# Moving the scores of one tile between the sums of the last image pair, transposing half of two lines unadded, and loading the last line as 120 and 8 partitions

## The chip, the cores and the metric

The kernel runs on one core of one Trainium2 chip. The metric is the device time of one execution in microseconds (us).

## The reference, cut to what matters

```python
# attention: q is 4 x 12288 x 128, kv is an image 4 x 384 x 32 x 128, r = 4
kv_pool = kv.reshape(B, H // r, r, W // r, r, C).mean(axis=(2, 4))   # 768 keys per batch
k = v = kv_pool.reshape(B, -1, C) @ w_sr
s = (q @ k.transpose(0, 2, 1)) / sqrt(C)
a = softmax(s)
x = a @ v
# feed-forward: d_ff = 1536
out = (maximum(x @ w_gate, 0) * (x @ w_val)) @ w_out
```

The pooling takes 4 x 4 pixels into one key. Each batch has 768 keys, which the kernel handles as three pairs of 128. A pair is loaded as four "lines" (the four pixel rows of the pooling window), each a copy of 128 partitions by 4096 bytes. Queries come in tiles of 512.

## The kernel before

TensorE pools and transposes at once: it transposes the pixels in float32 and accumulates the transposes in PSUM. VectorE halves the number of transposes by adding two lines first.

```python
def kv_load(b, pair):
    parts = work.tile([128, r, 2, r, C], FP32, tag="kv_in", bufs=3)
    rows = kv[b, pair * 2 * HC : (pair + 1) * 2 * HC].rearrange(
        "(hp dh) (wp h dw) c -> dh hp wp (h dw c)", dh=r, h=2, dw=r)
    for dh in range(r):                                   # four lines, 512 KiB each
        nc.sync.dma_start(parts[:, dh].rearrange("p h dw c -> p (h dw c)"), rows[dh])
    kv_in[b, pair] = parts

def turn_add(b, pair, lines, first=False, final=False, chunks=(0, 1)):
    n = lines.shape[2]
    for h in chunks:                                      # h: the two halves (128 keys each)
        for i in range(n):                                # four float32 transposes, accumulated
            nc.tensor.matmul(kv_Ts[b, pair][:, h], lines[:, h, i], ident, is_transpose=True, ...)
    if final and h == 1:                                  # copy from PSUM for the projection
        nc.vector.tensor_copy(kvT, kv_Ts[b, pair])
# ... cut ...
idle = bank([128, 128])                                   # warm-up of TensorE
for _ in range(34):
    nc.tensor.matmul(idle, ident16, ident16, start=True, stop=True)
# ... cut: tile 0, first pair of keys, start of the second pair ...
for k in range(GRP):                                      # four tiles of queries
    for jc in range(2, 4):
        scores(k, jc)                                     # second pair of keys
    if k == 0:
        turn_values(0, 1)
    if k == 1:
        turn_open(0, 2)                                   # third, last pair
        turn_add(0, 2, s2, first=True)                    # its lines 0 and 1, added before
        for h in range(2):                                # its lines 2 and 3, half by half
            s2 = add_lines(2, 2, nc.vector, slice(h, h + 1))
            turn_add(0, 2, s2, final=True, chunks=[h])
    if k == 2:
        project(0, 2)
attend(0, 1)
attend(1, 1)
for jc in range(4, NJC):
    scores(0, jc)                                         # third pair of keys
turn_values(0, 2)
for jc in range(4, NJC):
    scores(1, jc)
# ... cut: values of tile 0, its normalization, scores of tiles 2 and 3, x_turn_pe(0) ...
# ... then the steady loop: value, gate and output projections of one tile
#     beside the attention of a later one, to the end ...
```

The softmax here doesn't subtract the row's maximum and nothing guards it: scores larger than these inputs give would overflow.

## Time and profile before

| | before |
|---|---|
| device time, median of 6 runs | 1048.48 us (1047.68 to 1049.20) |
| the profiled execution | 1048.43 us, span 1046.4 us |
| TensorE busy | 1036.4 us, 99% of the span |
| from the first value projection (32.82 us) to the end | 1013.6 us |

The table says where a change can act: from 32.82 us on, TensorE is the bound (busy for 1009.47 of 1013.61 us), and the opening before it is 3% of the time. The prediction below shows the lines of the opening.

To compare openings between executions I use three marks from each trace. **A** is the start of the eight float32 transposes of the last pair's first two lines (22.62 in the prediction's timeline); up to there all kernels of this study do the same, apart from the warm-up where that is said. **B** is the last semaphore update of that pair's second line. **L** is the last update of its last line. (In these traces a 128-partition line has sixteen updates by DMA, for the second line of the profiled execution of before from 19.25 to 19.89 us. I call what one update reports a share, and read it as the part of one of the core's sixteen DMA engines: while only late shares were missing, from 22 to 23 us there, the DMA share is 0.06, about one of sixteen. "Fetch" is the transfer of the 16384-byte instruction block that the prediction shows.) The start of the first value projection, counted from A, is the length of the opening that the change can alter.

### The profile page before, as it was taken

The page shows a single profiled execution, that of the slowest core. Times are in us where ns is not written, and L with a number is a line of the kernel's source. Part 1 is how long each engine was busy: PE and PEld are TensorE (multiplying, and loading weights), DVE is VectorE, ACT ScalarE, POOL GpSimd, SP SyncE. Part 2 cuts the span into 40 slices and gives each one's busy share as a digit, 9 for nine tenths or more (in the row PEclk, how much of TensorE's full clock was granted, in tenths as well). Part 3 has the DMA queues.
Part 4 walks back from the last instruction along what each step waited for, and adds up shares of the span by engine and source line. Part 5 has one row for each costly group of instructions (what it writes and reads, how often), then busy time and mean ns, then how long its engine had stood idle before and what let it go on. Part 6 is the DMA issues. An engine that isn't in the chain of part 4 may idle for free.

```text
span 1046.4 us, 25971 instructions
## 1 busy us (share of the span) xinstructions
PE 1036.4 (99%) x9980; PEld 691.1 (66%) x9980; DVE 913.8 (87%) x1680; ACT 908.5 (87%) x1741; POOL 107.6 (10%) x127
## 2 busy tenths in 40 slices
PE   7999999999999999999999999999999999999998
PEld 6566666666666666666666666666666666666665
DVE  3788889898888888898888888889988888888898
ACT  2988888888888888888888888888888888888887
POOL 2000045200000015500000003430000000000000
PEclk9999999999999999999999999999999999999999
DMA  8833256231322335523224134551331322212111
GB/s 302 119 81 69 70 191 162 57 87 32 84 54 62 76 122 140 154 62 72 54 64 87 31 87 132 147 152 40 78 65 53 72 63 55 67 32 67 32 47 47
DMA packets 125853, 90.75 MB, mean 87 GB/s; under 512 B 103328, under 2 KB 104224, under 8 KB 125728
## 3 DMA queue, kind: packets, MB, share of 16 engines
q1 hardware_dynamic: 120288, 75.85, 26.8%
q0 software_dynamic: 5440, 13.24, 7.7%
q8 instruction: 78, 1.28, 0.5%
q14 instruction: 47, 0.39, 0.1%
HBM read 52.76 MB, written 25.17 MB: 74 GB/s over the span
## 4 chain that ended last, share of the span: by engine, by line
PE 97%; DMA 2%; SPq 0%; DVE 0%; ACT 0%; issue 0%; DVEq 0%; ACTq 0%
PE bank_ps L255 25%; PE bank_ps L234 24%; PE bank_ps L245 24%; PE bank_ps L196 12%; PE bank_ps L185 12%; DMA parts<-in_kv_dram 1%; DMA q<-in_q_dram 1%; PE bank_ps L166 0%; PE bank_ps L154 0%; SPq L128 0%; ACT val L238 0%; PE bank_ps L174 0%; PE bank_ps L227 0%; DVE kv_s L343 0%; DVE rinv L204 0%
## 5 line engine op out<-in xcount | busy, mean ns | idle before, releaser
L248 DVE SCALAR_TENSOR_TENSOR hT<-bank_ps,val 128x512 f16<-128x512 f32 x1152 | 759.6, 686 | 100.9 <-ACT val L238 74.5
L238 ACT CAST val<-bank_ps 128x512 f16<-128x512 f32 x1152 | 677.8, 591 | 112.1 <-PE bank_ps L234 107.5
L255 PEld LDWEIGHTS <-hT 128*128 128x128 f16 x4608 | 351.4, 98 | 199.9 <-issue 0.4
L255 PE MATMUL bank_ps<-wo,hT 128*128 128x128 f16 x4608 | 443.2, 219 | 0.0
L234 PE MATMUL bank_ps<-xT,wv 128*128 128x512 f16 x1152 | 436.6, 379 | 0.1
L245 PE MATMUL bank_ps<-xT,wg 128*128 128x512 f16 x1152 | 435.7, 378 | 0.1
L186 ACT ACTIVATE aT<-bank_ps 128x512 f16<-128x512 f32 x576 | 346.3, 605 | 18.4 <-PE bank_ps L185 18.4
L196 PE MATMUL bank_ps<-kv,aT 128*128 128x129 f16 x2304 | 223.3, 219 | 0.0
L196 PEld LDWEIGHTS <-aT 128*128 128x128 f16 x2304 | 177.3, 98 | 68.4 <-issue 0.4
L185 PE MATMUL bank_ps<-qT,kv 128*128 128x512 f16 x576 | 216.4, 379 | 1.5 <-DVE kv L167 0.8
L245 PEld LDWEIGHTS <-wg 128*128 128x128 f16 x1152 | 111.5, 97 | 66.1 <-issue 1.0
L234 PEld LDWEIGHTS <-wv 128*128 128x128 f16 x1152 | 112.7, 98 | 0.4 <-issue 0.4
L212 DVE TENSOR_TENSOR x<-bank_ps,rinv 128x256 f16<-128x256 f32 x188 | 79.7, 424 | 6.7 <-DVE rinv L204 0.2
L78 POOL DMA_DIRECT2D q<-in_q_dram x23 | 12.5, 543 | 571.8 <-DMA qT<-q 571.5
L273 DVE TENSOR_SCALAR o_sb<-bank_ps 128x512 f32<-128x512 f32 (+1 forms) x95 | 64.0, 673 | 1.3 <-PE bank_ps L255 1.3
L137 POOL TENSOR_TENSOR s<-parts 128x512 f32<-128x512 f32 x36 | 45.3, 1270 | 162.7 <-DMA parts<-in_kv_dram 122.3
L185 PEld LDWEIGHTS <-kv 128*128 128x128 f16 x576 | 55.9, 98 | 2.4 <-DVE kv L167 1.4
L204 DVE RECIPROCAL rinv<-bank_ps 128x2 f32<-128x2 f32 x192 | 30.5, 159 | 1.2 <-PE bank_ps L196 1.2
L139 POOL TENSOR_TENSOR s<-s 128x512 f32<-128x512 f32 x18 | 22.8, 1268 | 1.4
L141 POOL TENSOR_TENSOR c<-s 128x256 f32<-128x256 f32 x18 | 13.0, 725 | 1.4
L161 DVE COPY kvT<-bank_ps 128x256 f32<-128x256 f32 x12 | 5.0, 415 | 7.2 <-PE bank_ps L154 7.2
L154 PE MATMUL bank_ps<-ident,kv_s 128*128 128x128 f32 x50 | 7.8, 275 | 1.6 <-DVE kv_s L343 1.6
(37 smaller groups left out, 83.3 us busy)
## 6 DMA issues: line engine op xcount, KB each, us to landing
parts<-in_kv_dram SPq DMA_DIRECT2D x48, 512.0 KB, 6.1
out_dram<-o_sb SPq DMA_DIRECT2D x95, 256.0 KB, 2.1
q<-in_q_dram POOLq DMA_DIRECT2D x23, 512.0 KB, 5.2
xT<-x SPq DMA_TRANSPOSE x94, 2.5
q<-in_q_dram SPq DMA_DIRECT2D x1, 768.0 KB, 7.9
wv<-in_moe_w_val_dram POOLq DMA_DIRECT2D x2, 192.0 KB, 4.6
wg<-in_moe_w_gate_dram POOLq DMA_DIRECT2D x2, 192.0 KB, 5.1
wo<-in_moe_w_out_dram POOLq DMA_DIRECT2D x1, 384.0 KB, 9.9
```

Source lines behind the costliest of these rows:

```text
L137: eng.tensor_tensor(s2[:, i], parts[:, 2 * i, h], parts[:, 2 * i + 1, h], op=ALU.add)
L185: nc.tensor.matmul(s_ps, kv16[:, k // NST, jc, 0:C], qT_of(k), start=True, stop=True)
L186: nc.scalar.activation(aTs[k][:, jc, :], s_ps, AF.Exp, scale=qk_scale)
L196: nc.tensor.matmul(x_ps[:, i, :], aTs[k][:, jc, s * 128 : (s + 1) * 128], kv16[:, k // NST, jc, C : 2 * C + 1], start=(jc == 0 and i == 0) ...
L204: nc.vector.reciprocal(rinvs[k, half], x_banks[k, half][:, :, C : C + 1])
L212: nc.vector.tensor_tensor(x16s[k][:, 2 * half : 2 * half + 2, :], x_ps[:, :, 0:C], rinv.to_broadcast([128, 2, C]), op=ALU.mult,)
L234: nc.tensor.matmul(va_ps, wv16[:, fb * 128 : (fb + 1) * 128], xTs[k], start=True, stop=True)
L238: nc.scalar.copy(val, va_ps)
L245: nc.tensor.matmul(g_ps, wg16[:, fb * 128 : (fb + 1) * 128], xTs[k], start=True, stop=True)
L248: nc.vector.scalar_tensor_tensor(hTs[k][:, fb, :], g_ps, 0.0, vals.pop((k, fb)), op0=ALU.max, op1=ALU.mult)
L255: nc.tensor.matmul(o_ps, hTs[k][:, fb, s * 128 : (s + 1) * 128], wo16[:, fb, :], start=first, stop=(fb == NFB - 1), skip_group_check=True,)
L273: nc.vector.tensor_scalar(o_sb, o_ps, 1.0 / X_SCALE**2, None, op0=ALU.mult)
```

## The change: intent and diff

TensorE stood idle for 1.10 us while it waited for the last line, although scores of tiles 2 and 3 were ready to run. The new order puts the scores of tile 2 ahead of those sums and the scores of tile 3 after them. It also transposes one half of the last two lines raw, so that this half needs no VectorE addition first, and puts the values of tile 1 behind its scores. The split of the last line is meant to take work from one DMA engine: 120 partitions, then 8.

```diff
         for dh in range(r):
-            nc.sync.dma_start(parts[:, dh].rearrange("p h dw c -> p (h dw c)"), rows[dh])
+            whole = parts[:, dh].rearrange("p h dw c -> p (h dw c)")
+            if (b, pair, dh) == (0, NJC // 2 - 1, r - 1):
+                cut = 2 * HC // r - 2
+                nc.sync.dma_start(whole[: 4 * cut], rows[dh][:cut])
+                nc.sync.dma_start(whole[4 * cut :], rows[dh][cut:])
+            else:
+                nc.sync.dma_start(whole, rows[dh])
# ... cut: the loop over k shown above goes; scores_of(k, pair) is scores of both its blocks ...
+    scores_of(0, 1)
+    turn_values(0, 1)
+    scores_of(1, 1)
+    turn_open(0, 2)
+    turn_add(0, 2, s2, first=True)
+    scores_of(2, 1)
+    turn_add(0, 2, line(2, 2), chunks=[0])
+    turn_add(0, 2, line(2, 3), chunks=[0], final=True)
+    turn_add(0, 2, add_lines(2, 2, nc.vector, slice(1, 2)), chunks=[1], final=True)
+    scores_of(3, 1)
+    project(0, 2)
     attend(0, 1)
-    attend(1, 1)
-    for jc in range(4, NJC):
-        scores(0, jc)
+    scores_of(0, 2)
     turn_values(0, 2)
-    for jc in range(4, NJC):
-        scores(1, jc)
+    scores_of(1, 2)
+    attend(1, 1)
     attend(0, 2)
```

More of the change, by code (lines that the diff above doesn't have):

```diff
@@ L384, with scores_of @@
     project(0, 1)
-    for k in range(GRP):
-        for jc in range(2, 4):
+    def scores_of(k, pair):
+        for jc in (2 * pair, 2 * pair + 1):
             scores(k, jc)
-        if k == 0:
-            turn_values(0, 1)
-        if k == 1:
-            turn_open(0, 2)
-            turn_add(0, 2, s2, first=True)
-            for h in range(2):
-                s2 = add_lines(2, 2, nc.vector, slice(h, h + 1))
-                turn_add(0, 2, s2, final=True, chunks=[h])
-        if k == 2:
-            project(0, 2)
+    scores_of(0, 1)
[9 more added lines that the diff above has]
+    project(0, 2)
     attend(0, 1)
+    scores_of(0, 2)
+    turn_values(0, 2)
+    scores_of(1, 2)
     attend(1, 1)
-    for jc in range(4, NJC):
-        scores(0, jc)
-    turn_values(0, 2)
-    for jc in range(4, NJC):
-        scores(1, jc)
     attend(0, 2)
@@ L409 @@
         keep_values(0, half)
-    for jc in range(4, NJC):
-        scores(2, jc)
+    scores_of(2, 2)
     x_turn_pe(0)
-    for jc in range(4, NJC):
-        scores(3, jc)
+    scores_of(3, 2)
     attend(1, 2)
```

## The prediction

> **What bounds the kernel now.** First I read the busy shares and the chain that ended last on the profile page.
>
> ```profile
> PE 1036.4 (99%) x9980; PEld 691.1 (66%) x9980; DVE 913.8 (87%) x1680; ACT 908.5 (87%) x1741; POOL 107.6 (10%) x127
> PE 97%; DMA 2%; SPq 0%; DVE 0%; ACT 0%; issue 0%; DVEq 0%; ACTq 0%
> ```
>
> TensorE has work for 1036.4 of 1046.4 us and is 97% of the chain. Windows over 50 to 1000 us show it busy without a gap. So the time is TensorE's list of work plus the holes in it, about 10 us, and nearly all of these lie in the first 44 us. A change of the opening can win only holes. Next I read the chain of waits from 20 to 33.3 us, the part that the change touches.
>
> ```profile
> 12.22 11.65 DMA parts<-in_kv_dram
> ...
> 24.00 0.70 DVE kv_s L343
> 24.70 0.04 issue
> 24.75 1.27 PE bank_ps L154 x8
> ...
> 26.04 0.44 DVE kvT L161
> ...
> 26.61 0.67 PE bank_ps L166 x2
> 27.28 0.43 PE bank_ps L185 x2
> 27.71 0.91 PE bank_ps L196 x16
> 28.62 0.23 PE bank_ps L185
> ```
>
> Here the chain leaves TensorE: the last image line lands at 23.88, VectorE adds its first half (0.70), TensorE sums it (eight float32 transposes in two halves), VectorE copies, TensorE projects at 26.61. The timeline of TensorE shows the hole in front of those sums, in brackets:
>
> ```profile
> 22.62 1.03 PE L154 MATMUL bank_ps<-ident,kv_s 128*128 128x128 f32 x8
> 24.75 1.26 PE L154 MATMUL bank_ps<-ident,kv_s 128*128 128x128 f32 x8 [1.10 <-DVE kv_s L343]
> 25.84 0.59 PE L185 MATMUL bank_ps<-qT,kv 128*128 128x512 f16 x2
> 26.61 0.67 PE L166 MATMUL bank_ps<-kvT,w_sr_f 128*128 128x256 f32 x2 [0.18 <-DVE kvT L161]
> ```
>
> 1.10 us idle (it counts a drain; by starts TensorE is free at 23.49, so 1.26 us), while the scores of tiles 2 and 3, whose inputs were ready at 22, stand behind the sums in program order. Last, why does the line land so late? Windows of half a microsecond:
>
> ```profile
> 21.00:21.50 0.50, 0.17 (x1) 0.11 (x2) 0.27 (x1) 0.00 (x0) 0.50 (x1) 1.00 0.89 360
> 21.50:22.00 0.50, 0.50 (x5) 0.31 (x4) 0.00 (x0) 0.25 (x1) 0.50 (x2) 1.00 0.23 74
> 22.00:22.50 0.50, 0.36 (x3) 0.01 (x1) 0.29 (x1) 0.50 (x2) 0.50 (x2) 1.00 0.07 16
> 22.50:23.00 0.50, 0.50 (x5) 0.50 (x5) 0.00 (x0) 0.50 (x2) 0.50 (x2) 1.00 0.06 25
> ```
>
> The last two columns are the DMA share and GB/s. From 22 to 23 us the share is 0.06, one engine of sixteen: one straggler. The DMA view of 20.5 to 22 us has the reason, a packet of another queue:
>
> ```profile
> q8 instruction: 1, 0.02, 4.5%
> ```
>
> That packet (16384 bytes) starts at 20.63 and takes 1.08 us, where the 4096-byte rows take 0.16. By the semaphore updates, fifteen shares of the third line are there by 21.17 and the sixteenth at 22.80; of the last line fifteen by 22.41 and the sixteenth at 23.88.
>
> [...] The trace of before only has 128-partition copies, with 16 updates each[...]. [...] the trace shows one slow engine but not its number. [...] 78 packets of 16384 bytes on that queue, and by about 20 us TensorE has run some 256 instructions; so the straggler should come back at the same place. [...] Here the split is meant to drop one engine[...].
>
> **The change, part by part.** Everything up to TensorE's 23.49 us keeps its order (the build's lists confirm it). GpSimd and ScalarE keep their lists; SyncE gets one more load, VectorE one add of 0.69 less, TensorE four float32 transposes more (eight of raw lines replace four of sums for one half). Steps taken from starts in the trace: a pair of scores 0.43, four transposes 0.44 (0.109 each), eight value matmuls 0.45, the projection 0.51 to the next start.
>
> Split. Without it the last line stays at 23.88. With it the 120 rows are there by about 22.41, and two engines carry 4 more rows at 0.16 each: about 23.0 (estimate). The third line's straggler (22.80) stays. The extra issue waits for a load that landed at 13.49, long before.
>
> New order from 23.49: scores of tile 2 to 23.92; four transposes of the third line (landed 22.80) to 24.36; four of the last line to 24.80, which need it by 24.36; meanwhile VectorE adds the second half, 24.00 to 24.70 even with the line at 23.88; four transposes of that sum to 25.24. So TensorE should not wait for the image at all, and **the split is worth about nothing once the order is changed**: a line at 23.88 is still 0.4 us early for the direct transposes, and the add is just in time (24.75 against 24.80). It only buys a margin.
>
> Then: scores of tile 3 to 25.70, the copy from PSUM 25.46 to 25.90 (last transpose start plus 0.31 as before), projection at 26.04 against 26.61: 0.57 won. That is 1.26 of hole plus 0.17 of the small wait between the halves, less 0.44 for the added transposes and less 0.43, because only one pair of scores is now left after the sums to cover the copy, as before; the two scores of tile 2 had to be done anyway.
>
> After the projection, before had scores (0.43) and two value groups (0.91) and reached the scores of the last pair at 28.46. Now only one value group (0.45) is left there: free at 27.00, but the new keys are scaled at 27.17 (projection plus 1.13, from the rows of before), so a wait of 0.23 and a start at 27.23. The bank wait behind the first exponential (0.5 us in before) stays, so the block to the end of tile 1's scores is as long as before, 28.51; then the moved value group of tile 1, 0.45, and tile 0's group starts at 28.96 against 29.74, about 0.8 won. From there both orders are alike: sums, turn of tile 0, scores of tile 3, and the first value projection at about 32.0 against 32.82. ScalarE has twelve exponentials in this stretch at about 0.49; it now starts at 23.90 rather than 26.25, so it is no new bound. Weights land by 29.78, the next tile's transposed queries at 39.28, needed past 41.5: early enough.
>
> From 33 us on the list is the same and bound by TensorE, so the 0.8 us should reach the end: 1048.71 - 0.8 = 1047.9.
>
> **Rivals.** (a) *The straggler decides.* [...] it gets four rows more: line at about 24.5, add done 25.2, sums end 0.5 later, and 0.3 is won: 1048.4. [...] (b) *The holes move.* The waits for the copy, the projection and the banks come back elsewhere (before 33 us TensorE's holes after 23.49 sum to only about 2.4, and 0.44 of work is added); scores in flight hold banks that the next ones want. Against: the build's waits there are for exponentials done by 24.5. Value: 1048.5 to 1048.7. (c) *Earlier start, later stall.* From 42 to 50 us ScalarE is 100% busy and sets the pace. If it were tied to absolute time, the gain would be given back there; but its exponentials come forward by the same 0.8, so I expect it to shift. Value if wrong: 1048.7. (d) *The split is worth its full 1 us besides*, if unprofiled runs straggle worse than the profiled one: 1047.0.
>
> **Range and chances.** The whole hole is below 0.3% of the time; 2% would need 21 us, which no part of this stage holds. The three runs of before spread by 0.95 us, as much as the effect, and another chip or moment can shift by as much. Hence 1047.9, 1046.8 to 1048.9, with 99% within 2%.
>
> **What would show it.** Right: the hole of 1.10 before the float32 transposes is gone and no wait of TensorE for image lines over 0.1 us remains; TensorE's projection starts near 26.0; the scores of the last pair near 27.2; first value projection near 32.0; a span near 1045.6. Right on the split: fewer than 0.1 us change if it is undone. Wrong: a new wait of over 0.4 us on the exponentials' banks, or the first value projection unchanged, or moved but with the span unchanged (rival c), or the last line landing after 24.4 (rival a).

## The result, and the profile after

The change ran at a median of 1048.36 us (1047.77 to 1049.01, six runs) against 1048.48 us (1047.68 to 1049.20, six runs) for the kernel before. The ratio is 1.0000, with a 95% interval of 0.9987 to 1.0013: the same. Ratios here and below are the mean time of one kernel's fast runs over the mean of the other's of the same rounds, so not quite the ratio of the medians.

This first line of the profile page of the changed kernel answers to the one of before; each engine has its busy us, share of the span and instructions:

```profile
PE 1036.4 (99%) x9984; PEld 690.5 (66%) x9984; DVE 913.9 (87%) x1679; ACT 908.9 (87%) x1741; POOL 107.6 (10%) x127
```

TensorE has its four transposes more, VectorE one addition less, and the busy times are the same within 0.6 us. The span of this execution is 1047.1 us. Next is the chain of waits of the changed kernel in the opening (start, duration, what):

```profile
13.12 12.24 DMA parts<-in_kv_dram
25.55 0.70 DVE kv_s L349
26.30 0.67 PE bank_ps L160 x4
27.00 0.44 DVE kvT L167
27.57 0.68 PE bank_ps L172 x2
```

The chain still runs through the last image line, as before: the line, VectorE's addition, the sums, the copy, the projection. In the timeline of TensorE of the changed kernel (start, duration, group, and in brackets the idle time before it):

```profile
23.42 1.04 PE L160 MATMUL bank_ps<-ident,kv_s 128*128 128x128 f32 x8
24.29 0.59 PE L191 MATMUL bank_ps<-qT,kv 128*128 128x512 f16 x2
24.72 1.34 PE L160 MATMUL bank_ps<-ident,parts 128*128 128x128 f32 x8
26.30 0.66 PE L160 MATMUL bank_ps<-ident,kv_s 128*128 128x128 f32 x4 [0.24 <-DVE kv_s L349]
...
27.57 0.67 PE L172 MATMUL bank_ps<-kvT,w_sr_f 128*128 128x256 f32 x2 [0.18 <-DVE kvT L167]
...
33.52 0.38 PE L240 MATMUL bank_ps<-xT,wv 128*128 128x512 f16 x1
```

The hole of 1.10 us is gone, and a small one of 0.24 us is left; the eight raw transposes take 1.34 us where eight others take 1.04, which is another 0.3 us of waiting. A is at 23.42, 0.80 us later than in the profiled execution of before, and the projection and the first value projection are later too. From A to the first value projection it is 10.10 us, against 10.20 before. The rest, from there to the end, is 1013.57 against 1013.62 us.

So in this pair of traces the gain of 0.8 us did not arise at all. The line came late again. The last update of the second line, B, is at 20.80; of the last line the 120-partition copy has fourteen shares at 22.65 to 24.30 and its fifteenth at 25.36, and the 8-row piece is there, in two shares, at 24.91. Fifteen and two are the numbers that the split was built on. L is thus 4.56 us behind B, longer than the 3.99 us of before. These windows of the changed kernel (the last two columns are the DMA share and GB/s) show it:

```profile
21.00:22.00 1.00, 0.61 (x2) 0.20 (x2) 0.94 (x2) 0.00 (x0) 1.00 (x1) 1.00 0.94 213
22.00:23.00 1.00, 0.87 (x5) 0.42 (x6) 0.19 (x2) 0.45 (x1) 1.00 (x2) 1.00 0.67 193
23.00:24.00 1.00, 0.86 (x8) 0.71 (x7) 0.17 (x1) 1.00 (x3) 1.00 (x3) 1.00 0.20 66
```

From 21 to 22 us the DMA engines are 94% busy and move only 213 GB/s; in the window before it was 356. In the packets of the trace a 4096-byte row of this copy takes 0.2 to 0.3 us and up to 0.49, where it takes 0.16 in the 128-partition lines. Then one engine is left over again: it fetched an instruction block of 16384 bytes at 22.07 (1195 ns) and had seven rows of the last line still to do after it.

### The profile page after: what moved, and what is told of

It is laid out like the page before. It is cut to its first block, busy times and chain, and to the rows that moved or that the text cites. A ratio compares the mean times of both kernels' runs of the same rounds, so it can differ in the third digit from the quotient of the medians.

```text
span 1047.1 us, 25980 instructions
## 1 busy us (share of the span) xinstructions
PE 1036.4 (99%) x9984; PEld 690.5 (66%) x9984; DVE 913.9 (87%) x1679; ACT 908.9 (87%) x1741; POOL 107.6 (10%) x127
## 4 chain that ended last, share of the span: by engine, by line
PE 97%; DMA 2%; SPq 0%; DVE 0%; ACT 0%; issue 0%; DVEq 0%; ACTq 0%
PE bank_ps L261 25%; PE bank_ps L240 24%; PE bank_ps L251 24%; PE bank_ps L202 12%; PE bank_ps L191 12%; DMA parts<-in_kv_dram 1%; DMA q<-in_q_dram 1%; PE bank_ps L172 0%; PE bank_ps L160 0%; SPq L134 0%; ACT val L244 0%; PE bank_ps L180 0%; PE bank_ps L233 0%; DVE kv_s L349 0%; DVE rinv L210 0%
## 5 line engine op out<-in xcount | busy, mean ns | idle before, releaser
L150 POOL TENSOR_TENSOR kv_s<-c 128x128 f32<-128x128 f32 x18 | 8.2, 454 | 1.4
```

## The experiments

All kernels gave the right result.

**The parts alone, and an attempt to move the fetch.** My theory after the result was that the new order works, that the split is harmful, and that an instruction fetch of TensorE delays one DMA engine. The rival was that the order itself gains nothing. Four kernels were timed on one chip, with nine runs of before at a median of 1048.20 us.

The order alone, from the changed kernel:

```diff
-            (the split of the last line)
+            nc.sync.dma_start(parts[:, dh].rearrange("p h dw c -> p (h dw c)"), rows[dh])
```

> The new order with the last line loaded as 128 partitions. Two marks make runs comparable whose image stream starts earlier or later: A, the start of the eight float32 sums of the third pair's first two lines (22.62 us before, 23.42 after the change), and B, the last update of that pair's second line (19.89 before, 20.80 after). Theory 1 (the order is worth its 0.8 us, and the split took it back by landing the line late): the last line ends about 4.0 us behind B as before (4.56 with the change), no hole of TensorE over 0.25 us before the last sums, the first value projection starts about 9.4 us behind A (10.2 before, about 10.2 after the change), the time 0.8 us below before. Theory 2 (the holes only move, the split is neutral): the first value projection stays 10.2 us behind A and the time as before.

Measured: 1047.95 us (1047.65 to 1048.15), ratio 0.9994 (0.9981 to 1.0008). The timeline of TensorE with the order alone:

```profile
24.24 1.04 PE L154 MATMUL bank_ps<-ident,parts 128*128 128x128 f32 x8
25.23 0.66 PE L154 MATMUL bank_ps<-ident,kv_s 128*128 128x128 f32 x4
...
32.45 0.38 PE L234 MATMUL bank_ps<-xT,wv 128*128 128x512 f16 x1
```

A is at 22.94 and L at 24.36, 4.05 us behind B, as late as in the profiled execution of before. TensorE nevertheless waits for no line: no bracket stands before the sums. The first value projection is 9.51 us behind A. By starts, the last four transposes come 0.99 us behind the eight raw ones, where the second and third trace of the change have 0.87, so some 0.12 us of waiting is left. This is the case that the prediction worked out, and in the opening the order does what was expected. The 0.8 us expected in the total is not shown: the median is 0.25 us lower and the interval holds 1.

The split alone, in the kernel before:

```diff
-            nc.sync.dma_start(parts[:, dh].rearrange("p h dw c -> p (h dw c)"), rows[dh])
+            (the split of the last line)
```

> The old order with the last line as 120 and 8 partitions. Theory 1 (the split lands the line later): fifteen shares of the 120 rows spread over more than 1.2 us and their packets take 0.2 to 0.3 us rather than 0.16; last update about 4.5 us behind B; first value projection about 10.7 us behind A; time about 0.5 us above before. The change's own intent (the split avoids the delayed engine): last update about 3.1 us behind B, first value projection about 9.3 behind A, time about 0.9 us below before.

Measured: 1049.23 us (1048.48 to 1049.70), ratio 1.0006 (0.9994 to 1.0019). The interval holds 1, so a loss in the total is not shown. The timeline of TensorE with the split alone:

```profile
25.20 1.26 PE L160 MATMUL bank_ps<-ident,kv_s 128*128 128x128 f32 x8 [1.07 <-DVE kv_s L349]
...
33.28 0.38 PE L240 MATMUL bank_ps<-xT,wv 128*128 128x512 f16 x1
```

The hole that the split could have removed is 1.07 us, against 1.10 before. L is 3.79 us behind B, and the first value projection 10.18 us behind A (23.10). The split gains nothing in this trace. Neither expectation is met: L lies between the 3.1 and the 4.5 us expected.

A warm-up with fewer instructions, in the kernel before. In the prediction's trace the fetch comes after some 256 instructions of TensorE, so I expected that 25 fewer warm-up matmuls, each wider, would move it behind the lines. (Each matmul counts twice, as a weight load and a matmul, of which the page of before lists 9980 each, so this is 50 instructions.)

```diff
-    idle = bank([128, 128])
-    for _ in range(34):
-        nc.tensor.matmul(idle, ident16, ident16, start=True, stop=True)
+    fill = const.tile([128, T], FP16)
+    nc.vector.memset(fill, 1.0)
+    idle = bank([128, T])
+    for _ in range(9):
+        nc.tensor.matmul(idle, ident16, fill, start=True, stop=True)
```

> The kernel before, with the 34 warm-up matmuls of 128 columns replaced by 9 of 512 columns: 50 TensorE instructions fewer ahead of the image lines, about the same time of warm-up. If the late share of the last two lines comes from TensorE's own instruction block of 16384 bytes, which is fetched at about its 261st recorded instruction in both traces, the fetch comes behind the image stream (near 26 us), all shares of the last line land within 0.7 us, about 2.5 us behind B, and the first value projection comes about 8.7 us behind A; time 1.4 us below before. If one engine is slow by itself, the last line stays about 4.0 us behind B and the time as before.

Measured: 1047.76 us (1047.54 to 1049.28), ratio 0.9996 (0.9984 to 1.0009). The fetch did not go to 26 us as expected: it is at 21.32, when TensorE had started 206 recorded instructions, against 256 in the first trace of before. So the first block does not wait for the 256th. That the blocks are TensorE's fits their number (78 for 19960 recorded instructions of TensorE in before, 256 to each), and the third to fifth start at nearly the same instructions in both kernels (685, 941, 1197 in before, 695, 943, 1207 here). But the fetch came behind that engine's image rows, and no share of the line was late: L is 2.51 us behind B. The 1.4 us expected in the total is not shown. The timeline of TensorE with the old order and the wide warm-up:

```profile
23.07 2.00 PE L154 MATMUL bank_ps<-ident,kv_s 128*128 128x128 f32 x16
...
25.68 0.67 PE L166 MATMUL bank_ps<-kvT,w_sr_f 128*128 128x256 f32 x2 [0.18 <-DVE kvT L161]
...
31.89 0.38 PE L234 MATMUL bank_ps<-xT,wv 128*128 128x512 f16 x1
```

All sixteen transposes run in one piece, and the first value projection is 8.82 us behind A. With an early line the old order is shorter than the new order's 9.3 to 9.5.

The new order with the wide warm-up, without the split (the two edits above together):

> The new order, one load of 128 partitions, and the 9 wide warm-up matmuls. If TensorE no longer waits for the line in the new order, an earlier line brings it nothing: first value projection about 9.4 us behind A as in the run with the order alone, so 0.7 us later than with the old order and wide warm-up, because the four added float32 transposes and the moved value group stand in it for nothing. If the new order still waits for the line, it gains with the earlier line and comes under 9.0.

Measured: 1048.07 us (1047.96 to 1048.67), ratio 0.9998 (0.9985 to 1.0010). L is 2.49 us behind B, 1.56 us earlier than with the order alone, and the first value projection is 9.34 us behind A. An earlier line brings the new order little (9.51 to 9.34): it hardly waits for it any more.

**What the split does to the copy, and on which engine the fetch runs.** These were one look each, beside a run of before at 1047.89 us; they were run for their traces.

The whole change with the wide warm-up:

> The whole change plus the 9 wide warm-up matmuls, so that the fetch of the instruction block no longer stands in the image stream. If the 120 rows are slow by themselves, their packets take 0.2 to 0.3 us and the last line ends 3.6 to 3.9 us behind B, where the same order with one 128-partition load and wide warm-up had 2.5; the first value projection comes about 9.4 us behind A all the same, since the new order waits for nothing before 1.4 us behind A. If the fetch had made the line late in the changed kernel, it now ends about 2.6 us behind B.

Measured: 1048.27 us, 9.33 us from A to the first value projection. The fetch came after the rows of its engine. Yet L, with the 8-row piece, is 3.73 us behind B, where the unsplit line with the same order and warm-up had 2.49. So in this pair of traces the split copy lands over a microsecond later by itself, without a fetch among its rows. The new order hides that here.

The change once more, with no edit:

> The changed kernel itself once more, for a second trace. If the late line of the first trace is typical, the last line ends 3.8 to 4.6 us behind B, the fifteen shares of the 120 rows spread over more than 1.2 us, and the first value projection comes 9.6 to 10.1 us behind A. If it was one bad execution: about 3.1 behind B and 9.4 behind A.

Measured: 1047.85 us. The timeline of TensorE of this second trace of the change:

```profile
23.06 1.03 PE L160 MATMUL bank_ps<-ident,kv_s 128*128 128x128 f32 x8
23.93 0.59 PE L191 MATMUL bank_ps<-qT,kv 128*128 128x512 f16 x2
24.36 1.04 PE L160 MATMUL bank_ps<-ident,parts 128*128 128x128 f32 x8
25.23 0.60 PE L160 MATMUL bank_ps<-ident,kv_s 128*128 128x128 f32 x4
...
26.44 0.67 PE L172 MATMUL bank_ps<-kvT,w_sr_f 128*128 128x256 f32 x2 [0.18 <-DVE kvT L167]
...
32.39 0.38 PE L240 MATMUL bank_ps<-xT,wv 128*128 128x512 f16 x1
```

Here the change goes as worked out: no wait for the image, the projection 3.38 us behind A (3.42 predicted), the first value projection 9.33 us behind A (9.4 predicted). L is 3.79 us behind B: the line was as late as the worse of the two expected cases, and the opening as short as the better. The fetch (20.45, 1332 ns) cut in again, and eight rows of the last line follow it on its engine. That engine is therefore one of the fifteen of the large copy, and not the one that the split leaves out.

The last line as two copies of 64 partitions, in the old order with the wide warm-up, to tell "fifteen engines" from "not 128 partitions":

```diff
-                cut = 2 * HC // r - 2
-                nc.sync.dma_start(whole[: 4 * cut], rows[dh][:cut])
-                nc.sync.dma_start(whole[4 * cut :], rows[dh][cut:])
+                at = 0
+                for hps in (16, 16):
+                    nc.sync.dma_start(whole[4 * at : 4 * (at + hps)], rows[dh][at : at + hps])
+                    at += hps
```

> Old order, wide warm-up, the last line as two loads of 64 partitions each[...]. If rows are slow [...], its packets take about 0.3 us and the last line ends 3.5 to 3.9 us behind B. If the slowness of the 120 rows comes from using fifteen engines or from one more load, this one ends 2.5 us behind B as with one load.

Measured: 1048.99 us. The halves land 2.81 and 3.37 us behind B (3.5 to 3.9 expected), and while all engines work on them most rows take 0.25 to 0.34 us. These windows of this kernel answer to those of the change above:

```profile
21.00:22.00 1.00, 0.59 (x2) 0.19 (x2) 0.94 (x2) 0.00 (x0) 0.89 (x1) 1.00 1.09 254
22.00:23.00 1.00, 0.85 (x5) 0.42 (x6) 0.19 (x2) 0.43 (x1) 1.00 (x2) 1.00 0.51 131
```

From 21 to 22 us all engines are busy, and the rate is again far below the 410 GB/s that the whole lines reach in the profiled execution of before:

```profile
20.00:21.00 1.00, 0.67 (x2) 0.30 (x2) 0.83 (x2) 0.00 (x0) 0.97 (x1) 1.00 1.05 410
```

So rows are slow without a missing engine too, in this one look.

Why they are slow is not shown. In the next run a row of the 32-partition copies takes 0.16 us (at most 0.17), so more copies of fewer partitions were not slow as such there. But that run moves only half as much at a time (205 to 213 GB/s from 20 to 23 us, against the 410 above), so no run tells one cause from another.

The last two lines of the pair in four copies of 32 partitions each, in the kernel before. In the trace each such copy has eight shares, and the DMA engines are about half busy (0.51 to 0.53 from 20 to 23 us), which I read as eight of the sixteen engines. The expectation counts on eight: either the fetch runs on one of them, or on an engine that carries none of these rows.

```diff
+            if (b, pair) == (0, NJC // 2 - 1) and dh >= r - 2:
+                at = 0
+                for hps in (8, 8, 8, 8):
+                    nc.sync.dma_start(whole[4 * at : 4 * (at + hps)], rows[dh][at : at + hps])
+                    at += hps
```

> Old order, old warm-up, the third pair's last two lines as eight loads of 32 partitions[...]. It is slow on purpose (sixteen rows of 0.16 us per engine and line) and asks on which engine the instruction block is fetched. If on one of the eight, seven image packets are in flight beside the fetch, one image packet of 0.43 us or so follows it, and a share lands over 0.8 us after the others. [...] eight image packets stay in flight beside it and no share is late.

Measured: 1049.74 us; the line is late on purpose. Once only eight engines carry image rows, eight image packets stay in flight beside the instruction packet (for instance from 19.98 to 20.18), and no share is late because of it. So the fetch ran on an engine that these copies do not use. The trace does not number the engines, so which one it is, and whether it is the same as in the trace of the change above, where it is among the fifteen, is not shown. The split had assumed the one that the 120-partition copy leaves out.

**Is the opening of before always the same?** The first traces were one execution for each kernel. Two more executions of the kernel before, one more of the change with five timed runs, and an attempt at a better kernel.

The kernel before again, with no edit:

> The kernel before once more, for a second trace. A, which no kernel here changes, lay between 22.6 and 23.4 us in nine traces, and from the first value projection to the end all took 1013.56 to 1013.65. So the end should be A plus 10.2 plus 1013.6, with A anywhere in that range; if the second trace has A near 23.1, the first trace of before had a lucky start. The last line again 4.0 us behind B, with one late share, since one load of 128 uses the engine of the fetch. If the distance from A to the value projection differs from 10.2 by more than 0.3, single traces can't carry the comparison.

Measured: 1047.49 us. The timeline of TensorE of this second trace of before:

```profile
23.29 2.00 PE L154 MATMUL bank_ps<-ident,kv_s 128*128 128x128 f32 x16
...
25.90 0.67 PE L166 MATMUL bank_ps<-kvT,w_sr_f 128*128 128x256 f32 x2 [0.18 <-DVE kvT L161]
...
32.10 0.38 PE L234 MATMUL bank_ps<-xT,wv 128*128 128x512 f16 x1
```

This is the same kernel as in the prediction's timeline, and the hole of 1.10 us is not there. The fetch (21.28) came behind the rows of its engine, L is 2.50 us behind B, and the opening takes 8.81 us from A, where it took 10.20. By the expectation's own measure (more than 0.3 us apart), single traces can't carry the comparison. These windows of this execution show the difference in the stream:

```profile
21.00:22.00 1.00, 0.48 (x2) 0.08 (x2) 0.87 (x2) 0.00 (x0) 1.00 (x1) 1.00 0.81 311
22.00:23.00 1.00, 0.93 (x5) 0.42 (x6) 0.24 (x1) 0.57 (x2) 1.00 (x2) 1.00 0.16 66
```

The stream ends by itself in 22 to 23 us, and no engine is left over as in the prediction's windows.

The change timed, with no edit:

> The changed kernel, timed in five more rounds, and a third trace. If the second trace (9.33 from A to the value projection) is typical and the first (10.10) the odd one, about 9.4, and a time 0.5 to 0.9 us below before; if both happen equally, 9.4 or 10.1 and 0.3 to 0.6 us below. Either way within 2% and, with runs that differ by 1 us among themselves, probably inside the interval.

Measured: 1048.41 us (1047.37 to 1050.39) against 1048.17, ratio 1.0006 (0.9993 to 1.0018). From A to the projection 3.38, to the first value projection 9.33 us, the same as in the second trace of the change. The 0.3 to 0.9 us expected in the total did not show.

The old order's early sums with the wide warm-up, and with scores and values placed in the remaining holes:

```diff
     for h in range(2):                       # the sums of the last lines, as before
         s2 = add_lines(2, 2, nc.vector, slice(h, h + 1))
         turn_add(0, 2, s2, final=True, chunks=[h])
+    scores_of(2, 1)
     attend(0, 1)
+    project(0, 2)
+    scores_of(3, 1)
+    scores_of(0, 2)
+    turn_values(0, 2)
+    scores(1, 4)
     attend(1, 1)
+    scores(1, 5)
# ... cut: six values of tile 2 moved ahead of x_turn_pe(0) ...
```

> Wide warm-up, one load of 128, the old sums, and value matmuls moved into TensorE's remaining holes: tile 0's group into the wait for the copy, tile 1's into the wait for the first exponential's bank, tile 2's first four pairs into the wait for tile 0's normalization. Three waits of about 0.3, 0.3 and 0.4 us go: the first value projection comes about 7.9 us behind A (8.82 with wide warm-up alone, 10.2 before), and the time is some 2 us below before. If the banks held by tile 2's values or ScalarE's queue bind instead, it stays above 8.5.

Measured: 1047.50 us (1047.29 to 1048.12) against 1048.17, ratio 0.9996 (0.9983 to 1.0010). The opening is the shortest of all, 8.21 us from A, where 7.9 was expected. But from there to the end it takes 1014.09 us, 0.47 more than with the plain order and the same warm-up (1013.62). Part of the gain is given back a few us later, and the 2 us expected in the total did not come. This window is of this kernel (the first number after the length is TensorE's busy time):

```profile
36.00:38.00 2.00, 1.77 (x15) 0.97 (x13) 1.42 (x5) 1.61 (x4) 0.00 (x0) 1.00 1.99 192
```

and this one of the old order with the wide warm-up:

```profile
36.00:38.00 2.00, 2.00 (x20) 1.22 (x18) 1.42 (x3) 1.74 (x5) 0.00 (x0) 1.00 1.31 147
```

TensorE is idle for 0.23 us where the other was full; that is half of the 0.47, and I did not follow the rest. A version that beats both kernels is therefore not shown: it has the lowest median of the kernels that were timed in several rounds, but its interval holds 1.

The kernel before a third time, with no edit:

> The kernel before a third time. Its two traces differ: in one the instruction block is fetched in the midst of the image rows, the last line ends 3.99 us behind B and the first value projection starts 10.20 behind A; in the other the fetch comes behind that engine's rows, 2.50 and 8.81. If these two are the states of the kernel, the third trace shows one of them: 9.7 to 10.3 with one image packet of about 0.43 us after the fetch, or 8.8 without one. Anything between 9.0 and 9.6 would mean that the fetch doesn't set the opening of the kernel before.

Measured: 1047.71 us, one look, beside another run of before at 1048.33. The opening takes 9.46 us from A, between the two others. I had expected one of two states, and it is neither. The fetch (20.15) cut in and one share of the line is late again, but only by 0.66 us (the other fifteen by 22.73, the last at 23.39), so TensorE waits 0.36 us:

```profile
24.26 1.26 PE L154 MATMUL bank_ps<-ident,kv_s 128*128 128x128 f32 x8 [0.36 <-DVE kv_s L343]
```

In these traces the fetch costs the more, the less its engine has done of its rows, against the others, when it is served: here that engine's share of the second line came some 0.85 us ahead of B, in the first trace 0.08. In that first trace the block took 1.08 us, the next two rows on its engine 0.43 and 0.37 where others take 0.16, and the last share of the line landed 1.47 us after the other fifteen; in the second trace none was late.

**The traces side by side.** In us; "cut in" means that rows of the last line followed the instruction block on its engine.

| kernel | L behind B | fetch | A to projection | A to first value projection | from there to the end |
|---|---|---|---|---|---|
| before, as in the prediction | 3.99 | cut in | 3.99 | 10.20 | 1013.62 |
| before, third trace | 3.15 | cut in | 3.25 | 9.46 | 1013.62 |
| before, second trace | 2.50 | behind | 2.61 | 8.81 | 1013.63 |
| change, first trace | 4.56 | cut in | 4.15 | 10.10 | 1013.57 |
| change, second trace | 3.79 | cut in | 3.38 | 9.33 | 1013.56 |
| change, timed again | 3.86 | cut in | 3.38 | 9.33 | 1013.55 |
| order alone | 4.05 | cut in | 3.55 | 9.51 | 1013.63 |
| split alone | 3.79 | cut in | 3.97 | 10.18 | 1013.57 |
| old order, wide warm-up | 2.51 | behind | 2.61 | 8.82 | 1013.62 |
| order and wide warm-up | 2.49 | behind | 3.38 | 9.34 | 1013.63 |
| change and wide warm-up | 3.73 | behind | 3.38 | 9.33 | 1013.57 |
| wide warm-up, 64 + 64 | 3.37 | behind | 3.65 | 9.85 | 1013.65 |
| wide warm-up, holes filled | 2.52 | behind | 2.72 | 8.21 | 1014.09 |
| copies of 32 (late on purpose) | | no late share | 5.29 | 11.50 | 1013.26 |

## Why the prediction was right or wrong

**That nothing of 2% could come of it** was right, for the reason given (one reading was off, but nothing rests on it: of the 10 us of holes not nearly all lie in the first 44 us; in the window from 1000 to 1046 us TensorE is busy for 42.83 of 46, so about 3.2 lie there): TensorE is the bound for 1013.6 us, and these 1013.6 us are the same within 0.1 us in every row of the table but the last two. In those an opening that is still shorter gave 0.47 us back, and one that is much later caught up 0.36.

**What the new order does to the opening** was right in mechanism and size. The projection was to come 3.42 us behind A, and came 3.38 us behind in two of three traces of the change and 3.55 with the order alone. The first value projection was to be 9.4 us behind A, and came at 9.33 twice and at 9.51 with the order alone. The added transposes are really paid for: against an early line, the new order is 9.33 - 8.81 = 0.52 us longer than the old, of which the prediction's 0.44 us for four float32 transposes is the larger part.

**The 0.8 us of gain** was wrong as a forecast. The step that failed is the one in which the prediction said of the straggler that it "should come back at the same place". It took the late line of the one profiled execution, and with it the 1.26 us of hole at the head of the sum, for a constant of the kernel. Three traces of before have 10.20, 9.46 and 8.81 us (mean 9.49), the three of the change 10.10, 9.33 and 9.33 (mean 9.59). The subtraction 10.20 - 9.4 compared the new order with the worst of these three executions. The new order wins about 0.9 us against that one, 0.1 against the next, and loses 0.5 against the best. The change makes the opening depend less on the line, but its mean over three traces is no shorter than that of before.

**The split** was said to be "worth about nothing once the order is changed". In two of three traces of the change that holds: TensorE waits for no line. But its own estimate, the last line at 23.0 or B + 3.1, was missed: it came 3.79 to 4.56 us behind B. Two terms were wrong. The rows of the 120-partition copy were counted at the 0.16 us of a 128-partition copy, and took 0.2 to 0.3 and more. And the engine that the 120-partition copy leaves out was taken for the slow one; in the first two traces of the change the fetch ran on one of the fifteen engines of that copy (seven and eight rows of the last line followed it there), so it was not the one left out. In the first trace of the change both came together, slow rows and a late fetch (22.07), and the opening took 10.10 us. So the split is a cost that the order hid in two of three traces. Rival (a) had this last outcome nearly right by its time for the line (24.5, that is B + 4.6 there) but for another reason: it gave the delayed engine four rows more, while in that trace the 8-row piece was there by 24.91 and the last share, at 25.36, was one of the 120-partition copy. The sign that the prediction had set for it, the last line landing after 24.4, came up in the first trace (25.36) and just so in the third (24.44).

**Rival (b)**, holes that move elsewhere, is not what happened: no new wait on the exponentials' banks of over 0.4 us came up. A wait of 0.18 us for the copy from PSUM stays, as predicted. **Rival (c)**, that a shorter opening is given back later, is refuted for the change, since the rest keeps its length; it did happen in the kernel with the filled holes, where the rest grew by 0.47 us. **Rival (d)**, a further 1 us from the split, is refuted by the split alone.

**The totals.** The measured 1048.36 us lies in the predicted range of 1046.8 to 1048.9, but so does the kernel before with 1048.48, so the range holding says nothing of the 0.8 us; nor does it speak for rival (a) that its 1048.4 came so near. The 26 runs of before that stood beside another kernel have a mean of 1048.32 us with a standard deviation of 0.44, and 12 of the change 1048.49 with 0.79. The difference, 0.17 us, has a standard error of 0.24, so these runs show no difference; a gain of up to 0.3 us or a loss of up to 0.6 would not be excluded. The two repeats of before (1047.49 and 1047.71) are not among the 26; with them the difference is 0.22. The start of the image stream moves as much: A lies between 22.62 and 23.43 in these traces, and the profiled execution of before had the earliest. That is why the predicted absolute times (projection near 26.0, first value projection near 32.0, span near 1045.6) were missed in every trace of the change, by about 0.4 us or more.

**What stays open.** What decides when the fetch is served is not settled. From the third on, the blocks start about 256 instructions apart (685, 941, 1197 in before). Counted back, the first would be due at the 173rd, which starts at 14.89 us (an estimate), while it ran at 20.63. With the wide warm-up the 173rd starts at 18.78 and the fetch ran at 21.32. It may have waited behind image rows; that is an inference. With the wide warm-up it came behind the rows in all five traces, and with the narrow one in one of eight (leaving out the copies of 32 partitions), so the warm-up has something to do with it. How often the fetch cuts in when no profile is taken, which engine it uses, why the rows of the split copies are slow, and why A varies are open too.

## What to carry to other kernels

When a hole at the start comes from a late transfer, profile the same kernel two or three more times before counting the hole as a gain: here one kernel had it at 1.10, 0.36 and 0 us. Reordering work so that nothing waits for the late transfer made the opening steadier here (9.33 to 10.10 us in three traces, against 8.81 to 10.20), but whatever it adds (here 0.44 us of transposes) is paid in every execution, while the wait was paid in two of three. The load was best left at 128 partitions here: in the trace of the change, with 8 partitions cut off to spare one DMA engine, the rows of the other 120 took 0.2 to 0.3 us and up to 0.49, where those of a whole line took 0.16.
